# A fused attention and mixture-of-experts kernel: the code for rare surplus rows is moved to other places in the program

## The chip, the cores and the metric

The kernel runs on one core of a Trainium2 chip. The metric is the device time of one execution in microseconds (us); lower is better. The engines that matter here: TensorE (PE, with PEld for its weight loads and PEldq for its sequencer), VectorE (DVE), ScalarE (ACT), GpSimd (POOL), and SyncE (SP), which issues most of the DMAs. Each engine has a sequencer of its own that reads the engine's instructions in order; a branch on a value of the data is run by every engine's sequencer for itself.

## What is computed

Three layers in a row. An attention layer in which a query sees only the keys of its own cluster gives x with 1536 rows of 512. Two mixture-of-experts layers follow, each with 8 experts whose weights are 512 x 1024 and 1024 x 512. The diff touches the second of them:

```python
N, D, E, F = (1536, 512, 8, 1024);  capacity = N // E * 2        # 384
expert_idx = np.argmax(x @ w_gate, axis=1)                       # one expert for each row
gate_w = softmax(x @ w_gate)[np.arange(N), expert_idx]
# disp[e]: the rows of expert e in order, at most `capacity` of them
h = np.maximum(np.einsum('ecd,edf->ecf', disp, w1), 0.0)
y = np.einsum('ecf,efd->ecd', h, w2)
out[i] = gate_w[i] * y[expert_idx[i], pos[i]]                    # zero for a row that is not kept
```

How many rows an expert gets is known only while the kernel runs. With the inputs used here the second layer's experts get 218, 225, 108, 228, 232, 260, 99 and 166 rows by the reference's own arithmetic. Of the first two, the first half of the rows (batch 0) gives 117 and 113, the second half 101 and 112.

## The kernel before

The order of the instructions is written out by hand (`manual_schedule`): every engine runs its instructions in the order in which the program makes them. Weights come in as float32 in four chunks of 128 x 1024 (line 187, SyncE), and ScalarE and VectorE split each chunk into a high and a low part (lines 199 and 200); these splits are strewn between the other work by `tick` and `pass_time`. Every product is made of three: high by high, high by low, low by high.

The work of an expert is a `Job`. In the second expert layer, experts 0 and 1 are *small jobs*: each is done once for each half of the rows, with one tile of 128 rows, so that there are four, called here (0,0), (0,1), (1,0) and (1,1) by half and expert. Experts 2 to 7, called e2 to e7, are *wide jobs* with two tiles (256 rows). e7 is the last job of the program.

`work` runs one job. A wide job makes its first products for 256 columns at once (`wide1`, line 1072: 8 groups of 12 matmuls). Then stands the branch of line 1291 and 1292: if the expert has more than 256 rows, `extra_tile` does a third tile from start to end. Then come the loads of the weights that the job asks for in its middle, then the second products of the first tile (`second`, lines 1117 to 1119: 8 chunks f of three matmuls), then those of the second tile, in a branch (line 1304) that is taken if the expert has more than 128 rows. A small job makes its first products by `tile1` (lines 1095 to 1102) and its second ones by `second`, within which, after the second chunk, `rest` does a last piece of the first products.

`second` calls `pause` after every other chunk, and for these jobs `pause` is `step`: it may place weight splits on ScalarE and VectorE, issue the next job's gathers (line 1010, GpSimd) and place one tile of the next job's preparation (`prep`: four transposes on TensorE, line 1051, into a PSUM buffer named `tp`, then copies by ScalarE and VectorE, lines 1053 to 1056). At its end ScalarE takes the accumulator `l2` out of PSUM (line 1136) and GpSimd scatters the rows (line 1159). There are two buffers for `tp` and two for `l2`; a new tile of a name takes the buffer that was released first.

After the third small job, (1,0), stands the branch of line 1333: if one of the small jobs has more than 128 rows, up to eight extra tiles follow, two for each small job. Where a branch is not taken, each engine runs a few instructions in its place that mark the skipped work as done (EVENT_SEMAPHORE, and INC_SWDGE_SEM on GpSimd); these wait until that engine's earlier work is finished. The first expert layer has a branch of another kind (`overflow`, line 1445) inside the second products of its second job: ten loops, one for each job, each of which runs `slow_tile` as often as the counts ask for; it loads the job's weights anew for every tile.

Of the kernel before, what the change touches and what calls it, by code (L numbers as in the profile page):

```python
# [26 lines left out]
def kernel(  # L27
# [17 lines left out]
    nc = tc.nc  # L45
# [23 lines left out]
    NY = 4  # L69
# [11 lines left out]
    rt = ctx.enter_context(tc.tile_pool(name="rt", bufs=1))  # L81
# [907 lines left out]
    class Job:  # L989
# [12 lines left out]
        def rows_in(self, t):  # L1002

            if self.gated and t >= len(self.main):
                t = 2 + self.e % 2 if self.wide else 3
            return xgs[t]

        def gather(self, t, rows):
# [100 lines left out]
                fill()  # L1109
            return lambda: turn(1)  # L1110

        def second(self, t, rows, hh, hl, pause, before=None, inside=None):
            w2h, w2l = W[self.h + 1]
            cs = self.cols(t, rows)
            ps = p2.tile([128, Dm], F32, name="l2")
            for f in range(FC):
                nc.tensor.matmul(ps[:rows], hh[:, f, cs], w2h[:, f, :], start=(f == 0), stop=False)  # L1117
                nc.tensor.matmul(ps[:rows], hh[:, f, cs], w2l[:, f, :], start=False, stop=False)  # L1118
                nc.tensor.matmul(ps[:rows], hl[:, f, cs], w2h[:, f, :], start=False, stop=(f == FC - 1))  # L1119
                if f == 1 and inside and self is not jobs[1]:  # L1120
                    inside()
                if f % 2 == 1:
                    pause()
                if f == 3 and inside and self is jobs[1]:
                    inside()
            if self.last:
                y = my.tile([128, XW], F32, name="xe", bufs=2)
                nc.gpsimd.memset(y[:, Dm:], 0.0)
                nc.vector.scalar_tensor_tensor(y[:, :Dm], ps, self.g12[t][:, 1:2], xgs[2 + t][:, :Dm], op0=OP.mult, op1=OP.add)
            else:  # L1130
                y = my.tile([128, Dm], F32, name="y")
            if self.last:
                spawn(self.finish(t, y))
                return
            if self.gated:
                nc.scalar.activation(y[:rows], ps[:rows], AF.Identity, scale=self.gate[:rows, t:t + 1])
            else:
                nc.scalar.activation(y[:rows], ps[:rows], AF.Copy)  # L1138
            if before:
                before()  # L1140
            self.scatter(t, rows, y)
# [81 lines left out]
                    yield  # L1223
                yield from route2(b, lc, st["ps2"])

        def extra_tile(self, t, hh=None, hl=None):

            main = dict(self.__dict__)
            if not self.wide:
                self.gather(t, 128)  # L1230
                self.gate = my.tile([128, 4], F32, name="xgate2")
                self.xh, self.xl = [my.tile([128, DC, 128], F32R, name="y") for _ in range(2)]
                hh, hl = self.hidden()
            self.prep(t, 128)
            rest = self.tile1(t, hh, hl, lambda: None)
            self.second(t, 128, hh, hl, lambda: None, inside=rest)
            self.__dict__.update(main)

        def hidden(self):
            room, _, pool = P[self.kind]  # L1240
# [5 lines left out]
    def work(job, nxt, hook=None):  # L1246
# [41 lines left out]
        early()  # L1288
        if job.last:
            job.scale_first()  # L1290
        if job.wide and job.gated:
            with tc.If(job.count() > job.n):  # L1292
                job.extra_tile(len(job.main), hh, hl)
        if job.last and job.b:
            held.discard(2 * E + 1)
        for n in mid:
# [2 lines left out]
        for t, rows in job.main:  # L1299
            if t and t == len(job.main) - 1 and job.tail:  # L1300
                while todo:
                    fill()
                pass_time(0.6, 4)
                with tc.If(job.count() > t * 128):  # L1304
                    if rows <= 32:
                        job.second_few(t, rows, hh, hl)
                    else:
                        job.second(t, rows, hh, hl, lambda: None)
                clock["now"] += 4.5 if job.gated else 2.0
            else:  # L1310
                if job.last and t == len(job.main) - 1:
                    st["ahead"] = AH[job.b]
                inside = rest
                if job is jobs[1] and t == len(job.main) - 1:
                    def inside():
                        while not nxt.ready():
                            tick(0.3)
                        nxt.gathers()
                        fill()
                        while todo:  # L1320
                            fill()
                        assert not chunks
                        while wops:
                            wstep()
                        overflow()
                job.second(t, rows, hh, hl, step if job.wide or job.gated else tick, early if job.gated or job is jobs[0] else None, inside)
                early()
                if job.wide:
                    fill(False)
                    fill(False)  # L1330
        if job is split[-2]:

            with tc.If(cnts[1][E] > 128):
                for other in split:
                    with tc.If(other.count() > 128):
                        other.extra_tile(1)
                        with tc.If(other.count() > 256):
                            other.extra_tile(2)
        if job.last and job.b:
            held.clear()  # L1340
        for n in post:
# [101 lines left out]
    def overflow():  # L1443

        with tc.If(st["over1"] > 0):  # L1445
# [7 lines left out]
            for n, job in enumerate(jobs):  # L1453
# [4 lines left out]
                with tc.For_i(lo, end, 1) as i:  # L1458
                    slow_tile(job, i + job.col)

    def slow_tile(job, c):
        ix = my.tile([128, 2], I32, name="ix")
        nc.vector.tensor_copy(ix[:, 0:1], st["tok1"][:, bass.ds(c, 1)])
        nc.vector.tensor_copy(ix[:, 1:2], st["dst1"][:, bass.ds(c, 1)])
        xg = xgs[0]
        nc.gpsimd.indirect_dma_start(
            out=xg[:, :Dm], out_offset=None, in_=x_dram,
            in_offset=bass.IndirectOffsetOnAxis(ap=ix[:, 0:1], axis=0), bounds_check=T - 1, oob_is_err=False)
        ps = pt.tile([128, DC, 128], F32, name="tp")
        for c in range(DC):  # L1470
            nc.tensor.transpose(ps[:, c, :], xg[:, c * 128:(c + 1) * 128], ident)
# [3 lines left out]
        for cc in range(DC):  # L1475
            raw = stage.tile([128, 1024], F32, name="raw")
            nc.sync.dma_start(raw, halves[job.h][:, cc, :])
            for n in range(2):
                nc.tensor.matmul(pa[n], xT[:, cc, :], raw[:, n * 512:(n + 1) * 512],
                                 start=(cc == 0), stop=(cc == DC - 1))  # L1480
        hT = [mc.tile([128, Dm], F32, name=n, bufs=k).rearrange("p (c s) -> p c s", c=4) for n, k in (("part", NY), ("yt", NY - 1))]
        for n in range(2):
            hb = my.tile([128, 512], F32, name="y")
            nc.scalar.activation(hb, pa[n], AF.Relu)
# [5 lines left out]
        for g in range(4):  # L1490
# [7 lines left out]
        nc.scalar.activation(y, po, AF.Copy)  # L1498
        nc.gpsimd.indirect_dma_start(
            out=y_dram, out_offset=bass.IndirectOffsetOnAxis(ap=ix[:, 1:2], axis=0), in_=y,  # L1500
            in_offset=None, bounds_check=2 * T - 1, oob_is_err=False)

    mp = mc = None
    gt2 = rt.tile([128, NT, 4], F32, name="gt2")
# [188 lines left out]
```

## Time and profile before

| | us |
|---|---|
| median of 3 runs (lowest, highest) | 877.01 (875.16, 879.27) |
| the profiled execution | 877.53 |
| its span, first to last instruction | 875.8 |
| TensorE busy, share of the span | 838.8, 96% |
| VectorE, ScalarE, GpSimd busy | 541.9, 498.1, 280.9 |
| mean granted clock of TensorE, of full speed | 0.975 |

All times in the rows below are microseconds from the start of the span, durations in us where the row has a decimal point and in ns in the views of one line. A row of a timeline is: start, duration, engine, line, operation, tiles, shape, count, and in brackets how long the engine stood idle before it and what ended that. "issue" means that the view names nothing that was waited for. The second expert layer's jobs lie at: (1,0) from about 689 to 702, (1,1) to 722, e2 to 743, e3 to 767, e4 to 792, e5 to 828, e6 to 848, e7 to the end.

### The profile page before, as it was taken

The page shows a single profiled execution, that of the slowest core. Times are in us where ns is not written, and L with a number is a line of the kernel's source. Part 1 is how long each engine was busy: PE and PEld are TensorE (multiplying, and loading weights), DVE is VectorE, ACT ScalarE, POOL GpSimd, SP SyncE. Part 2 cuts the span into 40 slices and gives each one's busy share as a digit, 9 for nine tenths or more (in the row PEclk, how much of TensorE's full clock was granted, in tenths as well). Part 3 has the DMA queues.
Part 4 walks back from the last instruction along what each step waited for, and adds up shares of the span by engine and source line. Part 5 has one row for each costly group of instructions (what it writes and reads, how often), then busy time and mean ns, then how long its engine had stood idle before and what let it go on. Part 6 is the DMA issues. An engine that isn't in the chain of part 4 may idle for free. (4 is left out here: it accounts for less than half of the span.)

```text
span 875.8 us, 14860 instructions
## 1 busy us (share of the span) xinstructions
PE 838.8 (96%) x5371; PEld 748.1 (85%) x5371; DVE 541.9 (62%) x1110; ACT 498.1 (57%) x967; POOL 280.9 (32%) x465
## 2 busy tenths in 40 slices
PE   8899999999998989999999999999998988999997
PEld 6799999889987878989989898988987767888886
DVE  6888888989888656447444353535477337655270
ACT  5798988888998315445333343535344336555361
POOL 3445556447864021321302122033221112222110
PEclk9799999999999979999999999999899989999999
DMA  4005422411113035744644444458374318866250
GB/s 98 28 28 199 143 96 73 139 32 47 55 37 107 19 126 169 222 153 138 189 162 138 135 145 137 120 186 287 107 257 140 128 51 295 264 204 221 73 171 17
DMA packets 62189, 116.84 MB, mean 133 GB/s; under 512 B 13737, under 2 KB 25769, under 8 KB 62096
## 3 DMA queue, kind: packets, MB, share of 16 engines
q1 hardware_dynamic: 52832, 92.60, 33.1%
q0 software_dynamic: 9264, 23.06, 8.2%
q8 instruction: 51, 0.84, 0.4%
q14 instruction: 42, 0.34, 0.1%
HBM read 97.29 MB, written 23.74 MB: 138 GB/s over the span
## 5 line engine op out<-in xcount | busy, mean ns | idle before, releaser
L200 DVE TENSOR_TENSOR wl<-raw,wh 128x1024 fp32r<-128x1024 f32 x124 | 150.5, 1222 | 40.0 <-ACT wh L199 36.1
L1072 PE MATMUL l<-xh,wh 128*128 128x256 f32 (+1 forms) x508 | 156.4, 310 | 2.7 <-ACT xh L1053 1.2
L1072 PE MATMUL l<-xh,wl 128*128 128x256 f32 (+1 forms) x508 | 155.2, 308 | 0.2 <-DVE wl L200 0.2
L1072 PE MATMUL l<-xl,wh 128*128 128x256 f32 (+1 forms) x508 | 148.1, 307 | 0.0
L1117 PE MATMUL l<-wh,hh 128*128 128x512 f32 x328 | 137.1, 418 | 1.2 <-PEq L1445 0.4
L199 ACT ACTIVATE wh<-raw 128x1024 fp32r<-128x1024 f32 x124 | 128.9, 1053 | 4.9 <-DMA raw<-in_moe_w_dram 4.8
L1119 PE MATMUL l<-wh,hl 128*128 128x512 f32 x328 | 131.0, 399 | 0.0
L1118 PE MATMUL l<-wl,hh 128*128 128x512 f32 x328 | 130.4, 398 | 0.0
L1075 DVE SCALAR_TENSOR_TENSOR hl<-l,hh 128x256 fp32r<-128x256 f32 (+1 forms) x127 | 61.3, 484 | 98.4 <-ACT hh L1074 95.0
L1074 ACT ACTIVATE hh<-l 128x256 fp32r<-128x256 f32 (+1 forms) x127 | 55.1, 434 | 104.5 <-PE l L1072 102.9
L776 DVE TENSOR_TENSOR El<-et,Eh 128x384 fp32r<-128x384 f32 x192 | 101.2, 557 | 12.2 <-ACT Eh L775 10.0
L1072 PEld LDWEIGHTS l<-xh,wh 128*128 128x128 f32 x508 | 96.3, 190 | 6.2 <-issue 2.8
L744 DVE TENSOR_REDUCE nm<-st 128x1 f32<-128x768 f32 x96 | 91.4, 952 | 13.7 <-PE st L739 12.8
L1072 PEld LDWEIGHTS l<-xh,wl 128*128 128x128 f32 x508 | 96.1, 189 | 1.2 <-DVE wl L200 0.4
L775 ACT ACTIVATE Eh<-et 128x384 fp32r<-128x384 f32 x192 | 87.7, 495 | 12.5 <-PE et L770 12.2
L1072 PEld LDWEIGHTS l<-xl,wh 128*128 128x128 f32 x508 | 93.6, 188 | 0.2
L753 ACT ACTIVATE E<-st,nm 128x768 f32<-128x768 f32 x96 | 87.0, 907 | 8.2 <-DVE nm L744 7.9
L1159 POOL DMA_INDIRECT y_dram<-y,t1d x23 | 23.3, 1012 | 194.0 <-ACT y L1138 164.8
L770 PE MATMUL et<-identr,Er 128*128 128x128 f32 x576 | 72.6, 244 | 4.4 <-DVE El L776 2.4
L1119 PEld LDWEIGHTS l<-wh,hl 128*128 128x128 f32 x328 | 62.8, 191 | 15.0 <-DVE hl L1089 0.3
L770 PEld LDWEIGHTS et<-identr,Er 128*128 128x128 f32 x576 | 65.5, 142 | 11.0 <-DVE El L776 3.7
L1117 PEld LDWEIGHTS l<-wh,hh 128*128 128x128 f32 x328 | 62.8, 191 | 13.5 <-issue 1.5
(322 smaller groups left out, 1558.5 us busy)
## 6 DMA issues: line engine op xcount, KB each, us to landing
raw<-in_moe_w_dram SPq DMA_DIRECT2D x128, 512.0 KB, 4.5
vraw<-in_v_dram SPq DMA_DIRECT2D x16, 192.0 KB, 2.5
x_dram<-xp SPq DMA_DIRECT2D x8, 384.0 KB, 3.3
out_dram<-xg SPq DMA_DIRECT2D x1, 3072.0 KB, 10.2
y_dram<-xg SPq DMA_DIRECT2D x1, 3072.0 KB, 10.3
part<-y_dram SPq DMA_DIRECT2D x12, 256.0 KB, 3.7
yt<-y_dram SPq DMA_DIRECT2D x12, 256.0 KB, 3.9
x_dram<-part POOLq DMA_DIRECT2D x12, 256.0 KB, 3.7
```

The lines of the kernel that those rows point to most:

```text
L199: nc.scalar.activation(wh[:, cs], raw[0], AF.Copy)
L200: nc.vector.tensor_tensor(wl[:, cs], raw[0], wh[:, cs].bitcast(F32), op=OP.subtract)
L744: nc.vector.tensor_reduce(nm, ps, axis=AX.XY, op=OP.max, negate=True)
L753: made = nc.scalar.activation(E, st.pop(("S", i, j))[:, :, :HW], AF.Exp, bias=st.pop(("nm", i, j)), accum_out=st["Z", i][:, j:j + 1])
L770: ins = nc.tensor.transpose(ps[:, n * 128:(n + 1) * 128].bitcast(F32R), E[:, part, n * 128:(n + 1) * 128], identr)
L775: nc.scalar.activation(Eh[o], ps, AF.Copy)
L776: nc.vector.tensor_sub(El[o], ps, Eh[o].bitcast(F32))
L1072: nc.tensor.matmul(ps[:, :n], (w1l if k == 2 else w1h)[:, c, fs], (self.xl if k == 1 else self.xh)[:, c, :n], start=(m == 0), stop=(m == l ...
L1075: nc.vector.scalar_tensor_tensor(hl[:, f, :n], ps[:, :n], 0.0, hh[:, f, :n].bitcast(F32), op0=OP.max, op1=OP.subtract)
L1117: nc.tensor.matmul(ps[:rows], hh[:, f, cs], w2h[:, f, :], start=(f == 0), stop=False)
L1118: nc.tensor.matmul(ps[:rows], hh[:, f, cs], w2l[:, f, :], start=False, stop=False)
L1119: nc.tensor.matmul(ps[:rows], hl[:, f, cs], w2h[:, f, :], start=False, stop=(f == FC - 1))
```

## The change

Four edits. The branch of line 1333 with the small jobs' eight extra tiles is taken out. In its place, `overflow2` does a small job's rows beyond 128 by loops over `slow_tile`, one loop for each of the four small jobs, inside a branch of the same condition; it stands in the last job, e7, within the second products of its first tile, after the second chunk. `slow_tile` learns to read and write the second layer's tables and rows. The wide jobs' branch for a third tile moves from ahead of the second products into those of the first tile, after the fourth chunk and after the `pause` there; the middle loads of weights are now issued ahead of it. `second` takes a list of places and functions for this (`inside`), in place of one function.

```diff
-        def second(self, t, rows, hh, hl, pause, before=None, inside=None):
+        def second(self, t, rows, hh, hl, pause, before=None, inside=()):
...
-                if f == 1 and inside and self is not jobs[1]:
-                    inside()
+                for at, what in inside:
+                    if at == f and not self.wide:
+                        what()
                 if f % 2 == 1:
                     pause()
-                if f == 3 and inside and self is jobs[1]:
-                    inside()
+                for at, what in inside:
+                    if at == f and self.wide:
+                        what()
...
-        def extra_tile(self, t, hh=None, hl=None):
-
-            main = dict(self.__dict__)
-            if not self.wide:
-                self.gather(t, 128)
-                self.gate = my.tile([128, 4], F32, name="xgate2")
-                self.xh, self.xl = [my.tile([128, DC, 128], F32R, name="y") for _ in range(2)]
-                hh, hl = self.hidden()
+        def extra_tile(self, t, hh, hl):
+
             self.prep(t, 128)
             rest = self.tile1(t, hh, hl, lambda: None)
-            self.second(t, 128, hh, hl, lambda: None, inside=rest)
-            self.__dict__.update(main)
+            self.second(t, 128, hh, hl, lambda: None, inside=[(1, rest)])
...
-        if job.wide and job.gated:
-            with tc.If(job.count() > job.n):
-                job.extra_tile(len(job.main), hh, hl)
...
-                inside = rest
+                inside = [(1, rest)] if rest else []
+                if job.wide and job.gated:
+                    def extra():
+                        assert not any(n > job.h + 2 for n in W)
+                        with tc.If(job.count() > job.n):
+                            job.extra_tile(len(job.main), hh, hl)
+                    inside.append((3, extra))
+                if job is every[-1]:
+                    def beyond():
+                        assert not chunks and not wops and not todo
+                        overflow2()
+                    inside.append((1, beyond))
...
-        if job is split[-2]:
-
-            with tc.If(cnts[1][E] > 128):
-                for other in split:
-                    with tc.If(other.count() > 128):
-                        other.extra_tile(1)
-                        with tc.If(other.count() > 256):
-                            other.extra_tile(2)
...
+    def overflow2():
+
+        with tc.If(cnts[1][E] > 128):
+            m1 = rt.tile([128, len(split)], F32, name="ends2_m")
+            for n, job in enumerate(split):
+                nc.vector.tensor_copy(m1[:, n:n + 1], st["cnt2", job.b][:, job.e:job.e + 1])
+            nc.vector.tensor_scalar(m1, m1, 127.0, float(cap + 127), op0=OP.add, op1=OP.min)
+            ends = rt.tile([128, len(split)], I32, name="ends2")
+            nc.vector.tensor_copy(ends, m1)
+            nc.vector.tensor_scalar(ends, ends, 7, None, op0=OP.logical_shift_right)
+            for n, job in enumerate(split):
+                nc.vector.tensor_scalar(ends[:, n:n + 1], ends[:, n:n + 1], 1, None, op0=OP.max)
+                end = nc.values_load(ends[:1, n:n + 1], min_val=1, max_val=CT2)
+                with tc.For_i(1, end, 1) as i:
+                    slow_tile(job, i + job.col)
```

The rest of the diff lets `slow_tile` work for gated jobs: other tables, rows with their gate in the last columns, `xgs[1]` and `xgs[2]` for the hidden rows, the gate as ScalarE's factor, and `out` as the target. `overflow`, the loops of the first layer, keeps its place.

## Rows read from the trace of the kernel before

**Rows 1.** The page, part 1: busy time, share of the span, instructions.
```profile
PE 838.8 (96%) x5371; PEld 748.1 (85%) x5371; DVE 541.9 (62%) x1110; ACT 498.1 (57%) x967; POOL 280.9 (32%) x465
```
**Rows 2.** TensorE's waits, 690 us to end: waited for, total us, times, longest.
```profile
PE tp L1051 <- issue: 4.2, 3, 2.4
PE l L1095 <- issue: 2.2, 1, 2.2
PE l L1095 <- PEq L1333: 1.3, 1, 1.3
PE l L1095 <- ACT xh L1053: 0.8, 1, 0.8
...
PE tp L1051 <- DVEq L1292: 0.3, 1, 0.3
```
**Rows 3.** Instructions of line 1333 (690 to 720): ns min/median/max, first and last start.
```profile
L1333 PEldq COMPARE_BRANCH  x1: 3830/3830/3830, 699.3 to 699.3; - x1
...
L1333 POOLq INC_SWDGE_SEM  x1: 2214/2214/2214, 703.1 to 703.1; - x1
```
**Rows 4.** Timeline of TensorE, small job (1,0).
```profile
688.72 0.39 PE L1119 MATMUL l<-wh,hl 128*128 128x512 f32 x1
...
695.43 0.63 PE L1051 MATMUL tp<-ident,xg 128*128 128x128 f32 x4 [0.34 <-DMA xg<-x_dram,u1d]
695.81 0.48 PE L1117 MATMUL l<-wh,hh 128*128 128x512 f32 x1
```
**Rows 5.** Timeline of TensorE, end of (1,0) and small job (1,1).
```profile
701.63 0.40 PE L1119 MATMUL l<-wh,hl 128*128 128x512 f32 x1
703.34 0.47 PE L1095 MATMUL l<-wh,xh 128*128 128x512 f32 x1 [1.31 <-PEq L1333]
...
706.27 0.80 PE L1095 MATMUL l<-wh,xh 128*128 128x512 f32 x1 [2.22 <-issue]
...
715.10 0.48 PE L1117 MATMUL l<-wh,hh 128*128 128x512 f32 x1
```
**Rows 6.** Stretch: us, TensorE busy (instructions), granted clock, DMA share, GB/s.
```profile
706.00:707.00 1.00, 0.73 (x2) 0.50 0.00 0
```
**Rows 7.** Timeline of TensorE, wide job e2 around the branch of line 1292.
```profile
733.14 0.28 PE L1072 MATMUL l<-xl,wh 128*128 128x256 f32 x1
733.26 0.27 PE L1072 MATMUL l<-xh,wl 128*128 128x256 f32 x1
733.69 0.47 PE L1117 MATMUL l<-wh,hh 128*128 128x512 f32 x1
...
734.92 0.40 PE L1119 MATMUL l<-wh,hl 128*128 128x512 f32 x1
737.72 0.63 PE L1051 MATMUL tp<-ident,xg 128*128 128x128 f32 x4 [2.41 <-issue]
```
**Rows 8.** Instructions of line 1051, 736 to 738 (e2).
```profile
L1051 PEldq EVENT_SEMAPHORE  x2: 51/1994/3937, 733.7 to 737.8; - x2
```
**Rows 9.** Instructions of line 1292, 720 to 862, all wide jobs.
```profile
L1292 PEldq COMPARE_BRANCH  x7: 70/313/326, 731.3 to 856.5; - x7
...
L1292 PEldq EVENT_SEMAPHORE  x5: 51/51/51, 733.6 to 858.7; - x5
...
L1292 DVEq EVENT_SEMAPHORE  x5: 21/21/21, 737.6 to 859.6; - x5
```
**Rows 10.** Line 1445 (340 to 352), and the first product behind it in TensorE's timeline.
```profile
L1445 PEldq COMPARE_BRANCH  x1: 3494/3494/3494, 343.8 to 343.8; - x1
...
347.62 0.47 PE L1117 MATMUL l<-wh,hh 128*128 128x512 f32 x1 [0.40 <-PEq L1445]
```
**Rows 11.** GpSimd's timeline behind line 1333; its first gather's issue, us to landing.
```profile
703.03 1.03 POOL L1159 DMA_INDIRECT out_dram<-y,u1d  x1 [10.00 <-ACTq L1333]
706.31 1.03 POOL L1010 DMA_INDIRECT xg<-x_dram,u1d  x1 [2.26 <-issue]
...
xg<-x_dram,u1d POOLq DMA_INDIRECT x1, 3.7
```

More of the change, by code (lines that the diff above doesn't have):

```diff
@@ L1004, in rows_in @@
             if self.gated and t >= len(self.main):
-                t = 2 + self.e % 2 if self.wide else 3
+                t = 2 + self.e % 2
             return xgs[t]
@@ L1312, in work, with branch @@
                     st["ahead"] = AH[job.b]
-                inside = rest
+                inside = [(1, rest)] if rest else []
[10 more added lines that the diff above has]
+                    inside.append((1, beyond))
                 if job is jobs[1] and t == len(job.main) - 1:
-                    def inside():
+                    def branch():
                         while not nxt.ready():
@@ L1325, in inside @@
                         overflow()
+                    inside.append((3, branch))
                 job.second(t, rows, hh, hl, step if job.wide or job.gated else tick, early if job.gated or job is jobs[0] else None, inside)
@@ L1459, in overflow @@
                     slow_tile(job, i + job.col)
+    def overflow2():
[12 more added lines that the diff above has]
+                    slow_tile(job, i + job.col)
     def slow_tile(job, c):
         ix = my.tile([128, 2], I32, name="ix")
-        nc.vector.tensor_copy(ix[:, 0:1], st["tok1"][:, bass.ds(c, 1)])
-        nc.vector.tensor_copy(ix[:, 1:2], st["dst1"][:, bass.ds(c, 1)])
+        if job.gated:
+            tok = dst = st[job.tok]
+        else:
+            tok, dst = st["tok1"], st["dst1"]
+        nc.vector.tensor_copy(ix[:, 0:1], tok[:, bass.ds(c, 1)])
+        nc.vector.tensor_copy(ix[:, 1:2], dst[:, bass.ds(c, 1)])
         xg = xgs[0]
+        src = job.src if job.gated else x_dram
         nc.gpsimd.indirect_dma_start(
-            out=xg[:, :Dm], out_offset=None, in_=x_dram,
-            in_offset=bass.IndirectOffsetOnAxis(ap=ix[:, 0:1], axis=0), bounds_check=T - 1, oob_is_err=False)
+            out=xg[:, :XW if job.gated else Dm], out_offset=None, in_=src,
+            in_offset=bass.IndirectOffsetOnAxis(ap=ix[:, 0:1], axis=0), bounds_check=src.shape[0] - 1, oob_is_err=False)
         ps = pt.tile([128, DC, 128], F32, name="tp")
@@ L1480, in slow_tile @@
                                  start=(cc == 0), stop=(cc == DC - 1))
-        hT = [mc.tile([128, Dm], F32, name=n, bufs=k).rearrange("p (c s) -> p c s", c=4) for n, k in (("part", NY), ("yt", NY - 1))]
+        if job.gated:
+            hT = [xgs[1 + n][:, :Dm].rearrange("p (c s) -> p c s", c=4) for n in range(2)]
+        else:
+            hT = [mc.tile([128, Dm], F32, name=n, bufs=k).rearrange("p (c s) -> p c s", c=4) for n, k in (("part", NY), ("yt", NY - 1))]
         for n in range(2):
@@ L1497, in slow_tile @@
         y = my.tile([128, Dm], F32, name="y")
-        nc.scalar.activation(y, po, AF.Copy)
+        if job.gated:
+            nc.scalar.activation(y, po, AF.Identity, scale=xg[:, Dm:Dm + 1])
+        else:
+            nc.scalar.activation(y, po, AF.Copy)
+        to = out if job.gated else y_dram
         nc.gpsimd.indirect_dma_start(
-            out=y_dram, out_offset=bass.IndirectOffsetOnAxis(ap=ix[:, 1:2], axis=0), in_=y,
-            in_offset=None, bounds_check=2 * T - 1, oob_is_err=False)
+            out=to, out_offset=bass.IndirectOffsetOnAxis(ap=ix[:, 1:2], axis=0), in_=y,
+            in_offset=None, bounds_check=to.shape[0] - 1, oob_is_err=False)
     mp = mc = None
```

## The prediction

> **What bounds the kernel now.** I read the page first: TensorE is busy for 96% of the span [rows 1], so a change pays only where TensorE stands still or runs slowly, or where it takes work off TensorE. The diff takes no executed product away; it moves and removes branches. So the second view is the list of TensorE's waits over the stretch that the diff touches, from 690 us to the end [rows 2]. There are few: 1.3 and 2.2 us in the small jobs behind the branch of line 1333, 4.2 us in three "issue" waits of the transposes of line 1051, 0.3 us of the same transposes behind line 1292, and 0.8 us in the third tile that really runs. "Issue" only says that the view names no cause, so the third step is to find one, in the events of the sequencers.
>
> **Part 1: the branch of line 1333 goes.** It guards eight extra tiles of the small jobs, and it is not taken. TensorE's sequencer spent 3.83 us in that one compare-and-branch [rows 3]. TensorE started its last product before it at 701.63, the next one at 703.34, and then a second gap came until 706.27 [rows 5]; both gaps are code that is not there yet, since no other engine is waited for. A second price stands behind them: at 706 to 707 the granted clock is 0.50, the lower of the two levels (1.2 instead of 2.4 GHz) [rows 6], and the products took 0.63 to 0.80 us there. The whole price is read by comparing two jobs with the same code. In job (1,1) it took from 701.63, the last product of the job before, to 715.10, the first second product: 13.47 us [rows 5]. In job (1,0) the same steps ran from 688.72 to 695.81: 7.09 us [rows 4]. The difference is **6.4 us**. Both stretches hold the next job's first transposes; in (1,0) these waited 0.34 us for gathered rows, so up to 6.7 us could come back.
>
> What is late next? Gathered rows of the first wide job: GpSimd's scatter started at 703.03 and its first gather only at 706.31, since the branch left 2.21 us of semaphore work on GpSimd's queue [rows 3, 11]. Without it the gather can start when the scatter's own 1.03 us are over, near 704.1 (an estimate), and lands 3.7 us later [rows 11], at 707.8. TensorE wants those rows at 701.63 + 6.4 = 708.0. That is nearly level, so I take 6.4 and not 6.7. The weights of that job were fetched long before and are split in program order between TensorE's steps; they move along. Lower bound of this part: 3.5 us (the gaps of 1.3 and 2.2 alone, if the clock should fall all the same).
>
> **Part 2: the wide jobs' branch for a third tile moves from ahead of the first tile's second products to behind their fourth chunk.** In job e2 TensorE multiplied until 734.92 and then stood until 737.72 before the transposes for the next job [rows 7]. Its sequencer spent 3.94 us in one semaphore wait for them, from 733.7 [rows 8], and VectorE passed the not-taken side of line 1292 at 737.6, the first of five such [rows 9]. That is the cause. The transposes write a PSUM buffer that the skipped third tile used last in program order, so they wait until VectorE, which had weights to split first, marks the skipped work as done. In the changed kernel the next job's transposes (after the second and the fourth chunk) come ahead of this job's third tile in program order, so the wait is gone, and the skipped tile's marks are next needed a job later. The four waits are 4.2 + 0.3 = **4.5 us** [rows 2]; they lie on TensorE alone with nothing beside them, so all of it is on the path.
>
> Costs of the move. The branch itself makes TensorE drain: 0.43 us from 733.26 to 733.69 between the starts of two products where the pair before has 0.12 [rows 7], so 0.3 us, paid before and after alike. The weight loads of the job's middle (SyncE's queue) are now issued ahead of the branch; SyncE waits for nothing there, so that is nothing. ScalarE's and VectorE's splits after the fourth chunk queue behind the moved branch, and who waits for them is the next job's first products, some 3 us of second products and a second tile away. GpSimd passes the branch before its scatter as now. The accumulator of the open first tile stays in its PSUM buffer while a third tile uses the other; the second tile takes the buffer that was released first, the third tile's, so it waits only for ScalarE's mark at the branch, for which four chunks are cover (12 products; six took 1.2 us from 733.69 to 734.92 [rows 7], so some 2.8 us). If that cover is too short, a part of the 4.5 comes back: bound 0 to 4.5. In job e5, where the third tile runs, the 0.8 us behind ScalarE [rows 2] stays.
>
> **Part 3: the loops in the last job.** Behind the second chunk of the last job a not-taken branch over four loops is added. The trace has no such branch, so it is bounded by its neighbours. Small side: line 1292 skips one tile (60 products, each with a weight load) for 0.33 us at most, and this is hidden: in the last job the sequencer reaches the branch at 856.5 and has TensorE drained at 858.7 [rows 9]. Large side: line 1333 skips eight such tiles, 3.83 us. Near it: line 1445 skips ten loops of the very body added here and took 3.49 us, of which TensorE saw 0.40 as idle [rows 10]. Four loops hold 112 products with their weight loads and the loops' control; I take 3.49, the row with the same body. Its cover is the work queued on TensorE: 858.7 - 856.5 = 2.2 us; 3.49 - 2.2 leaves 1.3, and as line 1445, with products of the same kind ahead of it, left only 0.40, I take 1.0 us as bare. The job now has two drains instead of one: 0.3. Together **+1.3 us**; both ends: 0.3 (all hidden), and 6.4 (the full price of line 1333, with a second fetch and the low clock).
>
> The Trainium skill, page "Runtime: NRT & Kernel Launch", section "Instruction fetch mechanics", says that prefetch is sequential, and that a taken branch to a target outside the two-page window stalls for a fetch. By that, part 3 costs a fetch wherever four loops reach past that window. The same section gives TensorE room for 2048 instructions; by that figure neither line 1333 nor the new branch would cost anything, and part 3 would be 0.3. Line 1333 skips about 960 and cost 3.83 us [rows 3], so the trace speaks for the window and against the figure.
>
> **The sum.** The profiled execution took 877.53 us, 1.7 beyond its span of 875.8, and lies 0.5 above the median. 877.53 - 6.4 - 4.5 + 1.3 = **867.9 us**.
>
> **Rivals.** (a) *The 4.5 us go to another wait*: gathered rows, or ScalarE's mark at the moved branch, become what TensorE waits for in the wide jobs. For it: VectorE was up to 4 us behind TensorE in e2 (737.6 against 733.7) [rows 8, 9], and its backlog does not shrink. Against it: nothing else is waited for in the list of waits. 867.9 + 4.5 = 872.4. (b) *The price of line 1333 is only moved*: part 3 costs 6.4. For it: 3.5 us of bare gaps in one place brought the low clock. Against: line 1445, with more to skip, cost 0.40 bare and no second gap. 867.9 + 5.1 = 873.0. (c) *The low clock is not due to the gap*, or the gather is late by as much: part 1 gives 3.5, so 870.8. (d) *Slower*: the moved branches of the wide jobs land on code that TensorE does not hold. Place: behind the fourth chunk of the five wide jobs that skip; price 3.5 us each, the gaps of line 1333; with all five 867.9 + 17.5 = 885.4; from four on the kernel is slower than before (867.9 + 14.0 = 881.9), with three it is at 878.4. Against it: the skipped stretch is the same code as now, and each of its branches took 0.33 us at most [rows 9]. (e) *The change doesn't do what it says*: the loops or small extras run. They would need a small job of more than 128 rows; the branch of line 1333 went the not-taken way. No price, since no loop ran.
>
> **How the numbers follow.** Forecast 0.62, (a) 0.13, (b) 0.12, (c) 0.08, (d) 0.04, (e) 0.01. The range leaves out (d), (e) and a little at each end: below, 867.9 less 0.3 for part 1, less 1.0 for a hidden part 3, less the median's 0.5 and as much of scatter, 865.6; above, (b)'s 873.0 and a little, 873.3. About 0.5% is what a measurement of this kernel can tell from no change, here 4.4 us, so faster means below 872.6. The forecast and (c) are faster; (a) and (b) lie at the line, and I give them half each way: faster 0.82, same 0.14, slower 0.04.
>
> **What would show it.** Part 1: line 1333 is gone, no low clock in the stretch behind the small jobs, about 7 us from the last product of (1,0) to the first second product of (1,1). Part 2: no waits of the transposes of line 1051 in e2, e3, e4, e6; if (a) holds, their sum stands at other lines. Part 3: one compare-and-branch of some 3.5 us on TensorE's sequencer in the last job with about 1 us idle behind it; under (b) a second gap and a clock of 0.50. The prediction is wrong if the list of TensorE's waits from the small jobs on still holds more than about 5 us.

## The result, and the profile after

| | before | after |
|---|---|---|
| median (lowest, highest), same chip | 876.02 us (870.00, 882.24) | 869.76 us (865.10, 874.60) |
| ratio, 95% interval | | 0.9919 (0.9896 to 0.9942) |
| the profiled execution; its span | 877.53; 875.8 us | 868.02; 866.1 us |

The kernel became 0.8% faster, some 6.3 us. A second set of times of the same two kernels gave 871.03 against 876.41 us, 0.9939 (0.9915 to 0.9963). The time lies where it was forecast, but the gain is smaller than the 9.6 us of the sum. The profiled executions do differ by 9.5 us, which must not be taken for agreement: 3.3 us of that is there already at the loops' branch of the first layer (343.81 us before, 340.46 after), in code that the change leaves alone.

TensorE's waits of the kernel after, 690 us to the end (waited for, total us, times, longest), answer [rows 2]:

```profile
PE tp L1051 <- DMA xg<-x_dram,u1d: 2.2, 2, 1.8
PE l L1117 <- PEq L1309: 1.7, 2, 1.6
PE l L1117 <- PEq L1459: 1.1, 1, 1.1
PE l L1095 <- ACT xh L1053: 0.7, 1, 0.7
PE l L1072 <- DVE wl L200: 0.3, 1, 0.3
```

Of the list before, the 0.7 us of the third tile that runs and two small waits, for gathered rows and for a weight split, are left; waits of 1 to 2 us at three other places stand where the others were. The list holds 6.0 us in all, where the one before held 9.5; in a second trace of the same kernel it holds 4.7. The prediction had called itself wrong if more than about 5 us were left: by that sign it fails in this trace, at gathered rows and at the branches of the last job. (Lines moved: 1309 is the third tile's branch, 1296 the second tile's, 1459 the loops' in the last job, 1161 the scatter.) Part 1's stretch in TensorE's timeline of the kernel after, which answers [rows 5]:

```profile
698.20 0.39 PE L1119 MATMUL l<-wh,hl 128*128 128x512 f32 x1
698.42 0.39 PE L1095 MATMUL l<-wh,xh 128*128 128x512 f32 x1
...
704.78 0.48 PE L1117 MATMUL l<-wh,hh 128*128 128x512 f32 x1
```

And one us of it in the windows of the kernel after (us, busy time of TensorE, its weight loads, VectorE, ScalarE and GpSimd with instructions, granted clock, DMA share, GB/s), for [rows 6]:

```profile
702.00:703.00 1.00, 1.00 (x9) 0.82 (x8) 0.00 (x0) 0.03 (x1) 0.75 (x1) 1.00 0.41 63
```

6.58 us instead of 13.47, without a gap, with the clock at its upper level. The two branches in the last job of the kernel after, in the views of line 1459 and of line 1309 (engine, operation, count: ns min/median/max, first and last start):

```profile
L1459 PEldq COMPARE_BRANCH  x1: 3727/3727/3727, 844.7 to 844.7; - x1
```
```profile
L1309 PEldq COMPARE_BRANCH  x1: 2904/2904/2904, 848.8 to 848.8; - x1
```

TensorE's timeline of the kernel after, in e3 and in the last job:

```profile
744.59 0.63 PE L1051 MATMUL tp<-ident,xg 128*128 128x128 f32 x4 [1.75 <-DMA xg<-x_dram,u1d]
...
848.77 0.47 PE L1117 MATMUL l<-wh,hh 128*128 128x512 f32 x1 [1.09 <-PEq L1459]
...
851.95 0.47 PE L1117 MATMUL l<-wh,hh 128*128 128x512 f32 x1 [1.55 <-PEq L1309]
```

The loops' branch takes 3.73 us where 3.49 were forecast, and leaves 1.09 bare where 1.0 were. What was not forecast: the short third-tile branch behind it, 0.33 us at most before [rows 9], now takes 2.90 and leaves another 1.55 us idle.

A table by jobs tells more than the totals, since whole executions of one kernel spread by 1.4%. Each number is the time from a job's first product on TensorE to the next job's (for e7 to the end of the span), in one profiled execution:

| kernel | (1,0)+(1,1) | e2 | e3 | e4 | e5 | e6 | e7 |
|---|---|---|---|---|---|---|---|
| before | 32.7 | 21.4 | 24.1 | 24.8 | 36.3 | 19.3 | 28.2 |
| after | 26.0 | 19.0 | 25.4 | 23.7 | 37.0 | 18.4 | 31.5 |
| after_again | 26.0 | 19.0 | 25.1 | 23.6 | 36.9 | 18.4 | 31.2 |
| p1_no_branch | 26.0 | 24.7 | 25.1 | 24.5 | 36.8 | 18.8 | 28.9 |
| p1_again | 26.0 | 21.8 | 24.5 | 24.6 | 36.9 | 19.2 | 28.9 |
| p2_move_only | 31.9 | 18.9 | 24.6 | 23.5 | 36.2 | 18.3 | 28.2 |
| p2_other_banks | 31.3 | 18.8 | 24.9 | 23.5 | 36.5 | 18.3 | 28.6 |
| p2_gathers_ahead | 26.0 | 19.0 | 24.0 | 23.7 | 37.0 | 18.4 | 30.8 |
| p3_loops_out | 26.0 | 18.9 | 25.7 | 23.6 | 36.9 | 18.4 | 28.9 |
| p3_one_loop | 25.9 | 19.1 | 24.7 | 23.7 | 37.0 | 18.4 | 29.3 |
| p3_next_to | 25.9 | 19.0 | 24.8 | 23.7 | 37.0 | 18.4 | 34.3 |
| p3_loops_end | 26.1 | 19.1 | 24.0 | 23.7 | 36.9 | 18.4 | 31.3 |
| best | 25.9 | 19.0 | 24.0 | 23.7 | 36.9 | 18.4 | 31.3 |
| best2 | 26.0 | 19.1 | 23.8 | 23.7 | 36.9 | 18.4 | 29.4 |

### The profile page after: what moved, and what is told of

Same layout as the page of the kernel before. It is cut to its first block, busy times and chain, and to the rows that moved or that the text cites. A ratio compares the mean times of both kernels' runs of the same rounds, so it can differ in the third digit from the quotient of the medians.

```text
span 866.1 us, 14874 instructions
## 1 busy us (share of the span) xinstructions
PE 828.9 (96%) x5371; PEld 740.4 (85%) x5371; DVE 541.2 (62%) x1110; ACT 496.8 (57%) x967; POOL 283.5 (33%) x465
## 5 line engine op out<-in xcount | busy, mean ns | idle before, releaser
L1072 PE MATMUL l<-xh,wl 128*128 128x256 f32 (+1 forms) x508 | 155.8, 309 | 0.3 <-DVE wl L200 0.3
```

The costliest lines, as they stand in the source:

```text
L1072: nc.tensor.matmul(ps[:, :n], (w1l if k == 2 else w1h)[:, c, fs], (self.xl if k == 1 else self.xh)[:, c, :n], start=(m == 0), stop=(m == l ...
```

## The experiments

The changed kernel once more (no edit):

> The changed kernel once more, unchanged, for a second trace and for times beside those of the next kernels. Theory: the stretches that the change touches repeat (from the last but one small job's last product to the last small job's first one 6.6 us with the clock at 1.00; the second wide job 25.4 us with a wait for gathered rows of 1.8 us; the last job 31.5 us with idle times of 1.1 and 1.6 us), while stretches that it doesn't touch (the start of the last two jobs of the first layer, at 283 and 579 us) differ from one execution to the next by up to some us with the granted clock. Rival: the differences of those stretches belong to the kernel and repeat as well.

0.9939 (0.9915 to 0.9963). The stretches that the change touches repeat: 6.68 us, e3 25.1, e7 31.2, the two branches 3.68 and 2.68 us. The untouched ones do not: the first job of the first expert layer began at 286.64 instead of 283.21 us, and the last but one of that layer, from about 580 us on, took 41.2 instead of 38.8 us. So the table is read by jobs, and totals by their intervals.

**Part 1 alone: the branch is left out of the kernel before.**

```diff
-        if job is split[-2]:
-            with tc.If(cnts[1][E] > 128):
-                ...
```

> The kernel before without the branch for the small jobs' rows beyond a tile at the end of the last but one small job (L1333); those rows are left out, everything else stays. Theory (part 1 of the prediction): the stretch from the end of the last but one small job's products to the first ones of the last small job falls from 13.47 us to 6.6 to 7.1 us, the granted clock there is 1.00 and not 0.50, the whole is 6.4 to 6.9 us shorter than the kernel before, and the waits of the transposes at L1051 in the wide jobs stay. Rival: the low clock in that stretch has another cause and comes back, or the gathers are late: only 3.5 us are gained.

> The kernel before without the branch L1333 once more, for a second trace and more times. In its first trace the 6.7 us were gone from the two small jobs, but the whole was only 2.1 us shorter, because the granted clock fell to 0.50 for 6.6 us behind the wait of 2.7 us in the first wide job (24.65 us, where it has 21.4 with the clock at 1.00) and for longer in the stretch from 579 us. Theory: that wait is now the one that the low clock follows, and it does so again: the first wide job takes 24 to 25 us, and the whole is some 2 to 3 us less than the kernel before. Rival: which gap the low clock follows is chance of one execution: the first wide job takes 21.4 us with the clock at 1.00 and the times spread as widely as before.

In both traces the stretch is 6.6 us, and the two small jobs together fall from 32.7 to 26.0. Yet the forecast of 6.4 to 6.9 us for the whole kernel is missed: the totals are 0.9971 (0.9944 to 0.9998) and 0.9963 (0.9933 to 0.9992), some 3 us less. In the first trace the low clock had moved on to e2's wait, which part 1 leaves; in the second it had not. TensorE's timeline in e2, first trace:

```profile
731.36 1.08 PE L1051 MATMUL tp<-ident,xg 128*128 128x128 f32 x4 [2.70 <-issue]
```

The windows of the first trace, all of e2 and one us behind the wait (the clock is the third column from the end):

```profile
714.93:739.58 24.65, 21.45 (x129) 18.72 (x128) 16.15 (x23) 13.71 (x21) 4.94 (x4) 0.86 0.78 264
733.00:734.00 1.00, 1.00 (x4) 0.71 (x4) 0.75 (x2) 0.08 (x1) 0.00 (x0) 0.50 1.02 389
```

TensorE's timeline in e2, second trace:

```profile
726.11 0.63 PE L1051 MATMUL tp<-ident,xg 128*128 128x128 f32 x4 [2.65 <-issue]
```

The window of e2, second trace:

```profile
709.73:731.51 21.78, 18.62 (x130) 16.50 (x128) 16.15 (x23) 13.71 (x21) 4.94 (x4) 1.00 0.85 297
```

A wait of 2.70 us with the low clock behind it, one of 2.65 us without: in these two traces the length of the gap does not tell which one draws it, as the rival of the second run had it. The job lost 2.9 us by it. In both traces the wide jobs were a little longer besides (e2 to e7 of the second trace 155.8 us, before 154.1), e5 by 0.6 us and e7 by 0.6 us in each. Counted from the first product of (1,0) to the end of the span, the two traces take 184.7 and 181.8 us, before 186.8: 2.1 and 5.0 us less, on either side of the 3 us of the totals. Why e5 and e7 became longer is open.

**Part 2 alone: only the wide jobs' branch moves** (the small jobs' branch stays):

```diff
-        if job.wide and job.gated:
-            with tc.If(job.count() > job.n):
-                job.extra_tile(len(job.main), hh, hl)
...
+                    inside.append((3, extra))
```

> The kernel before with one move: in the wide jobs the branch for a third tile stands inside the second products of the first tile (behind its fourth step) instead of ahead of them. The branch at L1333 stays. Theory as forecast: all waits of the transposes on VectorE's mark go, 4.5 us less than the kernel before. Theory after the trace of the changed kernel: they go, but one wait for gathered rows of some 1.8 us comes in the job of the second wide expert, so 2.4 us less. Rival: the moved branch lands on code that TensorE doesn't hold, 3.5 us more for each job.

0.9948 (0.9922 to 0.9975), 4.6 us; e2 to e7 fall from 154.1 to 149.7 us, by 4.4. The forecast of 4.5 was right for the move by itself. This kernel also gives the price of the old branch a second time: the stretch of [rows 5] is 12.00 us here, with a shorter low clock, not 13.47.

**Part 2 without moving anything: the third tile's transposes write to other PSUM buffers.**

```diff
-            ps = tp()
+            ps = room() if (room := st.get("room")) else tp()
...
-                ps = pt.tile([128, DC, 128], F32, name="tp")
+                ps = st["room"]() if st.get("room") else pt.tile([128, DC, 128], F32, name="tp")
...
             with tc.If(job.count() > job.n):
+                st["room"] = lambda: p1.tile([128, 512], F32, name="l1").rearrange("p (c s) -> p c s", c=DC)
                 job.extra_tile(len(job.main), hh, hl)
+                st["room"] = None
```

> The kernel before, where only the third tile's transposes (in the branch that is nearly always skipped) write into PSUM buffers of the first products' pool instead of those that the transposes of the next job's rows use. The branch stays where it was. Theory: what held the transposes at L1051 was the mark of the skipped branch on its own PSUM buffers, which VectorE sets only when it comes to the branch; with other buffers those waits (2.2 to 2.4 us in the first wide jobs) go without any move, and the time is 2.4 to 4.5 us under the kernel before, as for the move alone. Rival: the place of the branch itself, its fetch or its draining, holds TensorE: the idle time stays, the time is that of the kernel before.

0.9938 (0.9912 to 0.9964). The branch stands where it stood, and the waits of line 1051 on the skipped tile are gone; TensorE's waits in this kernel, 690 us to the end:

```profile
PE l L1095 <- issue: 2.3, 1, 2.3
PE tp L1051 <- DMA xg<-x_dram,u1d: 1.4, 2, 0.9
PE l L1095 <- PEq L1335: 1.2, 1, 1.2
PE l L1095 <- ACT xh L1053: 0.7, 1, 0.7
PE l L1072 <- DVE wl L200: 0.2, 1, 0.2
```

e2, e4 and e6 are as short as with the move. So the skipped tile's claim on the `tp` buffers was the cause, not the branch's place, fetch or draining. The old branch of the small jobs is still in the list (1.2 and 2.3 us; the stretch is 11.90 us here).

**Why e3 waits for rows in the changed kernel: the gathers go ahead of the second tile's branch.**

```diff
+                if job.wide and job.gated and job in every[:-2]:
+                    every[every.index(nxt) + 1].gathers()
                 pass_time(0.6, 4)
                 with tc.If(job.count() > t * 128):
```

> The changed kernel, where a wide job issues the gathers of the job after the next between its first tile's scatter and the branch of its second tile, not behind that branch. Theory: what makes the second wide job's transposes wait 1.75 us for their rows is that GpSimd comes to those gathers 5.7 us behind the scatter when the second tile is skipped (2.34 us for the skipped scatter's mark and 3.4 us behind it) against 1.3 us when it is taken; issued ahead of the branch they start 1.1 us behind the scatter, the wait goes and the second wide job falls from 25.4 to 23.6 us: 1.5 to 1.8 us less than the changed kernel. Rival: the rows' transfer of 7 us beside the weights' transfers sets it, and the rows land no earlier than before: 0.

0.9924 (0.9892 to 0.9956). GpSimd's timeline behind e2's scatter, kernel after:

```profile
731.20 1.04 POOL L1161 DMA_INDIRECT out_dram<-y,u1d  x1 [12.86 <-ACT y L1138]
736.93 1.79 POOL L1010 DMA_INDIRECT xg<-x_dram,u1d  x1 [4.69 <-DVE hl L1075]
```

GpSimd's timeline behind e2's scatter, this kernel:

```profile
733.31 1.04 POOL L1161 DMA_INDIRECT out_dram<-y,u1d  x1 [12.87 <-DVE wl L200]
736.42 1.26 POOL L1010 DMA_INDIRECT xg<-x_dram,u1d  x1 [2.07 <-DVE hl L1075]
```

The gather starts 3.1 us behind the scatter, not 5.7. In the three kernels with this edit e3 takes 23.8 to 24.0 us; in the seven traces with the moved branch and without this edit 24.0 to 25.7, on average 24.9. So about 1 us is shown, not the 1.5 to 1.8 expected, and one of those seven (p3_loops_end) had its rows early enough as it was. What still holds GpSimd for 2.1 us behind the scatter is open: the view puts it down to VectorE's line 1075, and no run tests that.

**Part 3: the changed kernel without the loops** (surplus rows of the small jobs are left out):

```diff
-                if job is every[-1]:
-                    def beyond():
-                        assert not chunks and not wops and not todo
-                        overflow2()
-                    inside.append((1, beyond))
```

> The changed kernel without the loops in the last job: the small jobs' rows beyond a tile are left out. Theory: the jump over the loops took TensorE's code with it, and the short branch for the third tile right behind it paid for a second fetch; without the loops both idle times in the last job (1.09 and 1.55 us) go and that branch takes 0.2 to 0.35 us instead of 2.90: 2.6 to 2.9 us less than the changed kernel, some 9 us less than the kernel before. Rival: the 2.90 us belong to the third tile's branch in the last job itself: then only 1.1 to 1.3 us go, some 7.5 us less than the kernel before.

0.9904 (0.9870 to 0.9939). e7 takes 28.9 us instead of 31.2 to 31.5, and the third tile's branch is short again, as the view of its line in the last job says:

```profile
L1309 PEldq COMPARE_BRANCH  x1: 340/340/340, 847.9 to 847.9; - x1
```

So the loops cost 2.3 to 2.6 us, and the 2.90 us of that branch belong to them.

**One loop instead of four:**

```diff
-            for n, job in enumerate(split):
+            for n, job in enumerate(split[:1]):
```

> The changed kernel with one loop instead of four under the branch in the last job (the other three small jobs' rows beyond a tile are left out), at the same place. Theory: the price is that of a jump out of the code that TensorE holds; over one loop, some 80 instructions of TensorE, as over the third tile's branch, it stays inside: 0.2 to 0.4 us for both branches, no idle time, the last job takes 28.3 to 28.9 us. Rival: the price is that of a branch with loops in it (marks, drains), whatever their number: the branch takes 3.3 to 3.7 us again and the idle times stay.

The loops' branch in the view of its line, this kernel:

```profile
L1459 PEldq COMPARE_BRANCH  x1: 333/333/333, 842.1 to 842.1; - x1
```

The same kind of branch, over a quarter of the code, takes 0.33 us and not 3.73; the idle time behind it is 0.3 us, and the third tile's branch behind it takes 0.21 us. (e7 is 29.3 us in this single execution, not the 28.3 to 28.9 expected.) Marks and drains are not the price; the length of the jump is. The Trainium skill says in the page "Runtime: NRT & Kernel Launch", section "Instruction fetch mechanics", that a taken branch to a target outside the current two-page window must wait until that page has been fetched. The trace agrees (a block that is skipped is jumped over) in that the long jump waits (3.73 us) and the short one does not (0.33 us); how wide the window is, no run shows.

The fetches themselves lie in the profile, as DMA packets of 16 KB of kind "instruction" on queue q8. They are read here as TensorE's code, for two reasons: before any long jump, from 15.6 to 295.3 us of the kernel after, one comes for every 230 to 270 of its matmuls and weight loads; and behind the long jumps TensorE's sequencer goes on 1.3 to 1.4 us after such a packet has come. The view of DMA queues says of q8 (packets, MB, share of the 16 DMA engines' time), in the kernel after during the loops' branch (844.72 to 848.45) and during the third tile's branch behind it (848.81 to 851.71), and in the kernel before during the second gap behind line 1333 (703.34 to 706.27):

```profile
q8 instruction: 1, 0.02, 2.3%
```
```profile
q8 instruction: 1, 0.02, 2.6%
```
```profile
q8 instruction: 1, 0.02, 2.4%
```

So a long jump brings one packet and then, 0.74 to 0.76 us after the branch has ended, a second one. In six traces (before, after, after_again, p2_move_only, p2_other_banks, p2_gathers_ahead) TensorE stands for this second packet until 3.1 to 3.5 us after the long branch's end, whether a short branch follows (the 2.90 us of line 1309) or plain products (the 2.22 us behind line 1333). In p3_one_loop no packet comes during either branch.

**The loops' branch behind the third tile's branch** (and not ahead of it):

```diff
-                    inside.append((1, beyond))
+                    inside.append((3, beyond))
```

> The changed kernel with the branch over the loops directly behind the third tile's branch of the last job (both behind the fourth step) and not ahead of it. Theory: the second fetch (the third tile's branch took 2.68 to 2.90 us behind the loops' branch) comes of code that the first fetch displaced; with the short jump first, that branch takes 0.2 to 0.35 us, only the loops' branch costs, and the last job takes 29.7 to 30.1 us instead of 31.2 to 31.5. Rival: the jump back to straight code pays in any order, and behind the loops' branch the second tile's branch takes 2.7 us: no change.

The third tile's branch in the last job of this kernel, in the view of its line:

```profile
L1309 PEldq COMPARE_BRANCH  x1: 333/333/333, 847.0 to 847.0; - x1
```

The loops' branch, likewise:

```profile
L1459 PEldq COMPARE_BRANCH  x1: 3509/3509/3509, 850.8 to 850.8; - x1
```

TensorE's timeline around it:

```profile
850.26 0.39 PE L1119 MATMUL l<-wh,hl 128*128 128x512 f32 x1
854.74 0.47 PE L1117 MATMUL l<-wh,hh 128*128 128x512 f32 x1 [4.08 <-PEq L1459]
```

One us behind it, in the windows of this kernel:

```profile
856.00:857.00 1.00, 1.00 (x3) 0.75 (x3) 0.00 (x0) 0.00 (x0) 0.00 (x0) 0.50 0.00 0
```

The wait for the second fetch is gone, as the theory had it (its packet still comes, 0.77 us behind the branch, while TensorE runs on), but e7 takes 34.3 us, 3 more. My expectation missed the sequencer's lead. In the kernel after the sequencer reached the loops' branch at 844.7, while queued products kept TensorE busy until 847.7. Here it had to sit out the third tile's marks first, which wait for TensorE's last product; it came to the loops' branch at 850.85, when the last product had ended (850.26 + 0.39), so the whole fetch was bare: 4.08 us, and the low clock followed.

**The loops' branch at the very end of the program**, and with it (in `best`) the gathers ahead:

```diff
...
     for n, job in enumerate(every):
         work(job, every[n + 1] if n + 1 < len(every) else None, hooks.get(n))
+    overflow2()
```

> The changed kernel with the branch over the loops moved from the last job's first tile to the very end of the program, behind the last tile. There TensorE has 5.7 us left between its last product and the end (ScalarE's copy, the scatter's issue and its landing). Theory: the fetch of 3.7 us lies beside that tail; the last job falls from 31.5 to 28.3 to 28.9 us, as without the loops, 2.6 to 2.9 us less than the changed kernel. Rival: the branch's fetch on GpSimd or ScalarE begins only behind its own last work, and draining or the mark of the skipped scatters comes behind the last scatter: the tail grows by 1 to 4 us and the gain is eaten.

> Both of the last two edits in one kernel: the loops at the very end, and the gathers ahead of the second tile's branch. If both theories hold: 4.1 to 4.7 us less than the changed kernel, 864.5 to 865.5 us where that takes some 869.5. If only one holds, 1.5 to 2.9 us less; if neither, no change.

0.9916 (0.9887 to 0.9945) and 0.9901 (0.9861 to 0.9940), in both e7 31.3 us: nothing gained there, the rival's case. TensorE's fetch (4.1 us) lies beside the tail as meant, and its last product ends 2.4 to 2.7 us earlier within e7; but GpSimd's mark for the skipped scatters now comes behind the last scatter, which started at 858.82, and the end of the span moved from 5.7 us behind the last product to 8.3. The view of the branch's line in p3_loops_end:

```profile
L1454 PEldq COMPARE_BRANCH  x1: 4113/4113/4113, 853.8 to 853.8; - x1
...
L1454 POOLq INC_SWDGE_SEM  x1: 782/782/782, 861.9 to 861.9; - x1
```

**The loops' branch between ScalarE's copy of the last tile and its scatter**, with the gathers ahead (`second` calls `before` there):

```diff
...
+                if job is every[-1]:
+                    job.second(t, rows, hh, hl, lambda: None, overflow2)
+                    continue
                 with tc.If(job.count() > t * 128):
...
```

> The gathers ahead of the second tile's branch as in the run before, and the branch over the loops between ScalarE's copy of the last tile and that tile's scatter (the last tile is computed without a branch of its own, which is taken here anyway). Theory: there the fetch lies behind TensorE's and ScalarE's last work, and GpSimd goes through its part of the branch while it waits for ScalarE (4.5 us idle before the last scatter); the last job falls from 31.2 to 31.5 us to 28.2 to 28.9 us, with a tail of 5.7 us behind the last product and not 8.3, and the whole is 2.3 to 4.5 us less than the changed kernel, ratio to the kernel before some 0.989. Rival: the skipped scatter's mark still comes between the copy and the scatter, or the scatter waits for a mark that follows a landing: the tail grows again by 2 to 3 us.

860.49 us against 871.33 of the kernel before on that chip: 0.9881 (0.9847 to 0.9915), the lowest ratio of all. GpSimd does its mark while it waits for ScalarE, as the view of the branch's line says:

```profile
L1461 PEldq COMPARE_BRANCH  x1: 3695/3695/3695, 848.5 to 848.5; - x1
L1461 POOLq INC_SWDGE_SEM  x1: 762/762/762, 852.6 to 852.6; - x1
```

The last scatter in GpSimd's timeline of this kernel:

```profile
854.45 0.98 POOL L1163 DMA_INDIRECT out_dram<-xe,u1d  x1 [5.18 <-ACTq L1461]
```

e7 takes 29.4 us, 2 less than in the kernel after, with a tail of 6.4 us behind the last product. It misses 28.9 because the scatter waits for ScalarE's part of the branch: it starts 0.94 us behind the copy's end (853.51), where it was 0.28.

## Why the prediction was right, and where its steps were off

By the two traces of the kernel after, jobs (1,0) to e7:

| part | forecast | measured | from |
|---|---|---|---|
| 1 | -6.4 | -6.9 in this pair of traces; -5.3 to -6.9 over three executions with the branch | stretch 13.47, 12.00, 11.90 against 6.58 to 6.68 |
| 2 | -4.5 | -2.4 and -2.8 in the kernel after; -4.4 alone | e2 to e6: 125.8 against 123.4 and 123.0; p2_move_only |
| 3 | +1.3 | +2.6 and +2.3 | e7: 31.5 and 31.2 against 28.9 (p3_loops_out) |
| in no part | 0 | +0.7 | e7 without loops: 28.9 against 28.2 before |
| sum | -9.6 | -5.9 and -6.6 | (1,0) to the end: 186.8 against 180.9 and 180.2; the medians say -6.3 and -5.4 |

*Part 1.* The stretch came out as worked out, and the gather came in time: GpSimd issued it at 700.92, right behind the scatter (699.59), and nothing waited. Two things were off. The half of the 6.4 us that was low clock came from one execution; in three it is 1.8 to 3.4 us (the stretch less 6.6 us and less the two gaps of 3.3 to 3.5). And taken alone, part 1 gave the whole kernel only 3 us, in part because e5 and e7 become 0.6 us longer each once the small jobs' branch is out; the sum has no term for that. The rival (c), the low clock comes all the same, is right in this weaker form: it can turn up behind another gap. In the changed kernel e2's gap is gone too.

*Part 2.* The mechanism held and is shown twice, by moving the branch and by other buffers. The step that failed is "all of it is on the path", and it failed only beside part 1: for the move alone it held (-4.4). In the changed kernel rival (a) holds in part: e3's transposes, no longer held by VectorE's mark, wait 0.9 to 1.8 us for gathered rows, and e5 became 0.6 us longer (36.3 to 36.9), which is not the move's doing: with the move alone e5 took 36.2, and in both traces of part 1 alone 36.8 and 36.9. The prediction added parts 1 and 2 as if neither touched the other's jobs. The moved branches took TensorE's sequencer 0.07 to 0.35 us each in e2 to e6, so rival (d) fell.

*Part 3.* The fetch (3.73 us) and its bare part (1.09) were sized from line 1445 [rows 10] and are right. Missing from the sum is the second fetch: after a long jump the code that follows comes only with a second packet, and the next branch, with TensorE behind it, waited for that. The trace before had a second gap too, 2.22 us behind line 1333 [rows 5]; the prediction read it rightly as code that is not there yet, but left it to rival (b), because line 1445 has none. It is the same thing: in both places one packet of TensorE's code is fetched in the gap. Behind line 1445 a second packet comes as well, 0.75 us after the branch, but TensorE does not stand for it; that its work lay within the first packet is argued, not shown. By the row of line 1333 I should have added up to 2 us. No low clock followed; rival (b) was half true, in the second gap.

The forecast time is 1.9 us too low, and the gain 3.3 us too large; the other 1.5 us are the profiled execution before, 877.53, which lay that much above the median of 876.02.

## What to carry to other kernels

A branch that is not taken still claims its buffers: whoever uses them next waits for the slowest engine to pass the branch; a wait that the profile puts down to nothing ("issue") ahead of the next user of a buffer can be the sign (the "issue" wait behind line 1333 was another thing, code still to come), and either another order or other buffers cured it here. A jump over much code (four loops or eight tiles here) costs TensorE's sequencer 3.3 to 4.1 us, a jump over one loop or one tile 0.07 to 0.43. What needs the next packet of code right behind a long jump, be it a short branch (2.7 to 2.9 us here) or plain products (2.2 to 2.5 us), waits again. Put such a jump where each engine's work ahead of it covers that (behind the last product and ahead of the last scatter here), or keep less code under it. Where the clock makes whole executions differ by more than the edit, compare the stretch that the edit touches, in several traces, and check what the total says.

## What the runs showed of the hardware that was not expected

- A gap's length alone does not tell whether the low clock follows: TensorE was idle for 2.41, 2.65 and 2.70 us in e2 of three traces with the same code in that job, and only at the last did the granted clock fall to 0.50, the lower level, where it stayed for 6 to 7 us. What decides it is open.
- TensorE's pace differs by kernel where nothing is waited for: in e5, 96 products of 256 columns start over 10.8 us in the kernel before and in p2_move_only, over 11.3 us in the kernel after and in both traces of p1_no_branch, 4% more; e7 takes 28.2 us in the first two and 28.9 in p1_no_branch and p3_loops_out. p2_other_banks has 11.2 and 28.6. Over these products the granted clock is 1.00 and no gap of TensorE exceeds 0.15 us in the kernels before and after. The cause is open; nothing was tried for it.
- GpSimd's mark for a skipped scatter takes 0.36 to 2.35 us; in e2, where it takes 2.34, the gather behind it starts 5.7 us after the scatter, against 1.3 us where the second tile runs (756.87 to 758.18 in the kernel after).
